# Group loads in two transfers from a six-part layout, and the maxima's transpose two places earlier, in an attention and Fourier-mixing kernel

## The chip, the cores and the metric

The kernel runs on one core of a Trainium2 chip. A core has TensorE (PE in the profile; PEld is its weight load), VectorE (DVE), ScalarE (ACT), GpSimd (POOL), and SyncE (SP), which issues the transfers; 16 DMA engines carry them out. The metric is the device time of one execution in microseconds. Before the change three runs took 1027.07, 1029.34 and 1030.61 us; the median is 1029.34.

## The reference

Two independent parts are computed and set side by side in the output (2048 rows, 2 x 576 columns, float32).

- Part A is attention with a compressive memory: 32 heads of 18 columns, 2048 positions in 4 segments of 512. In each segment there is causal softmax attention, `p = softmax(q k^T * scale + mask)`, `a_dot = p v`; from segment 1 on also a lookup in a memory matrix that the earlier segments filled, `a_mem = phi(q) M / (phi(q) z)`. The two are mixed by a gate per head, `g * a_mem + (1 - g) * a_dot`, and multiplied by `wo`. The mask is `ar[:, None] < ar[None, :]`, so a query sees keys up to its own position.
- Part B is a Fourier mixing layer on another input: `a = x Wd_re`, `b = x Wd_im` along the 576 columns, then `y = Ws_re a - Ws_im b` along the 2048 positions, with the DFT matrices given as inputs.

Float32 accuracy is kept on bfloat16 and reduced-float32 matmuls by splitting a number into a high part and remainders. In the scores, q and k are each split into three bfloat16 parts, and six of the nine products are kept: part pairs (0,0), (0,1), (1,0), (0,2), (2,0), (1,1).

## The kernel before, in words

**Projections (lines 435 to 480, about the first 230 us).** For each segment s, nine products `project_qk(s, m)` make q (m = 0 to 3) and k (m = 4 to 7) in transposed form, 128 columns at a time; m = 8 holds the last 64 columns of both. Each is split into three bfloat16 parts in a tile `p` (four buffers, L244): ScalarE makes part 0, VectorE the remainder r, ScalarE or GpSimd part 1, GpSimd part 2 (L258). One transfer writes `p` into a DRAM tensor `qd[s]` or `kd[s]` of shape 576 x 3 x 512 (L260 to L263). Then `project_v` makes v and writes it to `vd[s]`. In parallel the memory of the segment is accumulated.

**Attention with the DFT in between (L815 to L896).** From about 240 to 940 us PE works off two streams. One is attention: 128 pairs of segment and head, n = 0 to 127, four to a group G = n // 4, 32 groups, eight per segment. The other is part B's matmuls (`dense()`, L583), a stream of long accumulating products on chunks `craw` that are loaded (`c_load`, L372, four buffers), split by ScalarE into `chi` (L387) and by GpSimd into `clo` (L392).

The generator `attention()` runs over pieces p = 0 to 67. A piece takes about 10 us, handles one even and one odd pair at different stages, and is cut into eight slots by `yield`. After each slot, matmuls of the dense stream are put in until its share is level. So the order on every engine is fixed by hand: the order of the calls in the source is the order of each engine's queue, and an engine runs its queue strictly in order. `later(n, ...)` puts a call n slots on (`tick`, L84). All transfers, with `dma = nc.sync.dma_start` (recorded as L87 when put off), go through SyncE's one queue: a transfer that must wait, or that takes long to issue, holds up all behind it.

- *Stacks.* For each group two tiles hold q and k with the six part products side by side in the contraction: `qs` and `ks`, 128 partitions x 4 heads x 512, of which 6 x 18 = 108 partitions are data (`NPAIR`). There are four buffers of each. `stack_load` (L419) fills a group with 12 transfers, one for each product and side: 18 partitions x 4 heads x 1 KB, 72 KB each. In piece p, odd, after `f_turn`, it puts off the last 4 of group (p + 3) // 2, two in a slot; in an even piece the first 8 of group (p + 4) // 2 (L859 to L862). A group is first used in piece 2G.
- *Even pairs* go as: scores (`s_fill`, L683) only for each row's maximum, taken by VectorE (L680); after both even pairs of a group, `maxima` (L721) splits the maxima into three bfloat16 parts on GpSimd; `maxima_transpose` (L729) turns them on PE (`trm`), ScalarE copies the result (`mt`), and two small transfers of 3 KB, put off by one slot, write it to partitions 108 to 110 of `qs` (L735). `ks` holds ones there, so that the next score matmul (`t_fill`, L737, 111 partitions) gives transposed scores with the maximum taken off, ready for exp and for the value product. `t_fill` of a group's first even pair stands in slot 1 of piece 2G + 3, three pieces after its `s_fill`.
- *Odd pairs* are computed by rows (`f_fill`, `f_exp`), split in two fp16 parts (`f_split_hi` on ScalarE, `f_split_lo` on GpSimd and VectorE, L714), and turned by a DMA transpose (`f_turn`, L719), one in a piece, issued by SyncE as well.
- *Value products.* `pv` (L775) puts an even and an odd pair into one PSUM bank, the tag `pv` with one buffer. `pv_out` (L793) empties it with four VectorE instructions (L803 to L806) at the end of the piece; the next `pv` follows in slot 3.
- *Score banks.* PSUM tiles with the tags s and t alternate between two banks each (`bank`, L489). Before the change `trm` is one of the t tiles, so an even piece uses five of them and an odd one four.

The slots of a piece that matter here, in the order of the source: slot 0 `s_fill` 0 (L837), slot 1 `t_fill` 0 and 1 (L840), slot 2 `s_fill` 1 (L844), slot 3 in even pieces `maxima_transpose` (L848), then `pv` of the even pair (L849); slot 4 `f_fill` 1, `t_fill` 2 and in odd pieces `maxima`; slot 5 `f_turn` (L858), `stack_load`, `f_fill` 0; slot 6 `pv` of the odd pair, `f_fill` 2; slot 7 `f_exp` and `pv_out` (L874).

**Output (from about 960 us).** Part A's rows are joined, turned and multiplied by `wo` (L903 to L919).

Of the kernel before, what the change touches and what calls it, by code (L numbers as in the profile page):

```python
# [15 lines left out]
BF16 = mybir.dt.bfloat16  # L16
AF = mybir.ActivationFunctionType
OP = mybir.AluOpType
# [4 lines left out]
S, D, H, DH, NSEG, L = 2048, 576, 32, 18, 4, 512  # L23
P = 128
# [4 lines left out]
HEAD0 = [0, 7, 14, 21, 24]  # L29
NPAIR = 108  # L30
BF16_ONES = float(np.array([0x3F803F80], np.uint32).view(np.float32)[0])
QPARTS = [0, 0, 1, 0, 2, 1]
KPARTS = [0, 1, 0, 2, 0, 1]


@with_exitstack
def infini_attention_and_fnet(ctx: ExitStack, tc: tile.TileContext, xT, wqk, w8, wv, wo, beta, xtT, cT, hT, out):
    nc = tc.nc
    act, dve, pool, pe = nc.scalar, nc.vector, nc.gpsimd, nc.tensor
    dma = nc.sync.dma_start  # L40
    ctx.enter_context(tc.manual_schedule())
    const = ctx.enter_context(tc.tile_pool(name="const", bufs=1))
    dram = ctx.enter_context(tc.tile_pool(name="dram", bufs=1, space=DRAM))
    wide = ctx.enter_context(tc.tile_pool(name="wide", bufs=32))

    qd = [dram.tile([D, 3, L], BF16, name=f"qd{s}") for s in range(NSEG)]
    kd = [dram.tile([D, 3, L], BF16, name=f"kd{s}") for s in range(NSEG)]
    vd = [dram.tile([P, 4, 8, 220], BF16, name=f"vd{s}") for s in range(NSEG)]
    amd = [dram.tile([P, D], F32, name=f"amd{t}") for t in range(NT)]
    yd = [dram.tile([P, D], F32, name=f"yd{t}") for t in range(NT)]  # L50
# [30 lines left out]
    def later(n, fn, *a):  # L81
        due.setdefault(clock[0] + n, []).append((fn, a))
# [7 lines left out]
    p1, p1k = ExitStack(), ExitStack()  # L90
    sk = p1k.enter_context(tc.tile_pool(name="sb1k", bufs=1, side="right", reuse_waits="tile"))
    sb = p1.enter_context(tc.tile_pool(name="sb1", bufs=1, reuse_waits="tile"))
    ps = p1.enter_context(tc.tile_pool(name="ps1", bufs=2, space=PSUM))
# [91 lines left out]
    for i in range(2):  # L185
        kn.append(tuple(sk.tile([P, D], F32R, name=f"kn{n}{i}") for n in "hl"))
        a, b = (sk.tile([P, H, 19], F32R, name=f"vn{n}{i}") for n in "hl")
# [3 lines left out]
        t = sb.tile([P, H, 55], BF16, name=f"vs{i}")  # L191
# [29 lines left out]
    def open_qk(s):  # L221
# [4 lines left out]
        for a, b in zip(edges, edges[1:]):  # L226
# [5 lines left out]
            if s and a == 0:  # L232
                accumulate(3, (0, 1))

    def project_qk(s, m):
        if m in FIRST:
            o = FIRST.pop(m)
        else:
            o = ps.tile([P, L], F32, name="qk", tag="acc", bufs=4)
            chain(o, qk_terms(s, m))  # L240
        if m >= 4 and s < 3:
            KF[m] = sk.tile([P, L], F32, name="kf", bufs=5)
            act.activation(KF[m], o, AF.Copy)
        p = sb.tile([P, 3, L], BF16, name="p", bufs=4)  # L244
        r = sb.tile([P, L], F32, name="r", bufs=2)
        act.activation(p[:, 0], o, AF.Copy)
        dve.tensor_tensor(r, o, p[:, 0], OP.subtract)
        if s and (m < 4 or m == 8):
            n = P if m < 4 else 64
            c = m if m < 4 else 4  # L250
            phi(sb, "q", o[:n], n, pq_hi[:n, c], pq_lo[:n, c])

        def rest():
            if m in (5, 6, 7):
                pool.tensor_copy(p[:, 1], r)
            else:
                act.activation(p[:, 1], r, AF.Copy)
            pool.tensor_tensor(p[:, 2], r, p[:, 1], OP.subtract)  # L258
            if m < 8:
                later(1, dma, (qd if m < 4 else kd)[s][(m % 4) * P:(m % 4 + 1) * P], p)  # L260
            else:
                later(1, dma, qd[s][4 * P:], p[:64])
                later(1, dma, kd[s][4 * P:], p[64:])  # L263

        later(1, rest)

# [96 lines left out]
    def h_split(ri, k):  # L363
        if k == 0:
            HW[ri] = weight(wide_tile(D))
        split_wk(HW[ri], k, HRAW.pop((ri, k)), 2 * ri)
# [30 lines left out]
    qs_bufs, ks_bufs, VS = [], [], {}  # L397
# [18 lines left out]

    NG = 32

    def stack_load(G, a, b, each):  # L419
        if G < NG:  # L420
            s, g8 = divmod(G, 8)
            rows = slice(g8 * 72, g8 * 72 + 72)
            for n in range(a, b):
                c = n // 2
                buf, src, part = ((ks_bufs, kd, KPARTS[c]), (qs_bufs, qd, QPARTS[c]))[n % 2]
                later(1 + (n - a) // each, dma, buf[G % 4][18 * c:18 * c + 18],
                      src[s][rows, part, :].rearrange("(h d) t -> d h t", d=DH))

    def value_load(G):
        if G < NG:  # L430
# [4 lines left out]
    for s in range(NSEG):  # L435
        more = s < 3
        if s == 0:
            warm_up()
        open_qk(s)
        if s:  # L440
            memory()
        else:
            tick()
        for n, m in enumerate((0, 1, 2, 3, 8, 4, 5, 6, 7) if s else range(9)):
            project_qk(s, m)
            tick()
            if not more and n >= 5:
                h_split(0, n - 5)
            if s in (1, 2) and n >= 4:
                load_x(s + 1, n - 4)  # L450
            if not more and n == 0:
                for k in range(5):
                    h_load(0, k)
            if not more and n == 4:
                p1k.close()
                sr = ctx.enter_context(tc.tile_pool(name="sb2r", bufs=1, side="right", reuse_waits="tile"))
                attention_tiles()
            if not more and n == 4:
                stacks(sr, 0)
                stack_load(0, 0, 12, 2)  # L460
            if not more and n == 5:
                c_load(0)
            if not more and n == 6:
                stacks(sr, 1)
        for j in range(4):
            project_v(s, j, lookup(s, j) if s else iter(()))
            if more:
                k_natural(j)
            tick()
            for k in ((0, 1), (2, 3), (4,), ())[j] if s == 0 else ():  # L470
                load_x(1, k)
            if more and j in (1, 2):
                split_x(s + 1, j - 1)
            if not more and j < 3:
                h_split(0, 4) if j == 0 else c_cut(j - 1, dve)
            if not more:
                c_load(1 + j)
            if more and j:
                accumulate(j - 1)
# [4 lines left out]
    ps = ctx.enter_context(tc.tile_pool(name="ps2", bufs=2, space=PSUM, reuse_waits="tile"))  # L484
# [4 lines left out]
    def bank(name, shape, dtype, tag):  # L489
        turns[tag] ^= 1  # L490
        return ps.tile(shape, dtype, name=name, tag=f"{tag}{turns[tag]}", bufs=1)
# [235 lines left out]
        pool.tensor_tensor(b[:, 2], r, b[:, 1], OP.subtract)  # L727

    def maxima_transpose(G):  # L729
        t = bank("trm", [P, P], BF16, "t")  # L730
        pe.transpose(t, MB[G % 2], ident16)
        w = sa.tile([24, P], BF16, name="mt", bufs=2)
        act.activation(w, t[:24], AF.Copy)
        for h in range(2):
            later(1, dma, qs_bufs[G % 4][NPAIR:NPAIR + 3, 2 * h].rearrange("c (n t) -> c n t", n=4), w[12 * h:12 * h + 12])  # L735
# [79 lines left out]
    def attention():  # L815
        for p in range(NP + V_LAG):
            def even(lag, fn, *a):
                if 0 <= p - lag < NP:
                    fn(2 * (p - lag), *a)

            def odd(lag, fn, *a):
                if 0 <= p - lag < NP:
                    fn(2 * (p - lag) + 1, *a)

            if p < 2:
                stacks(sa, p + 2)
            if p == 0:
                value_load(0)
                stack_load(1, 0, 12, 2)
            if p % 2 == 0:  # L830
                later(39, value_load, p // 2 + 1)
            if p == NP + 1:
                o_load(0)
                o_load(1)
            even(T_LAG + 1, t_lo, 0)
            odd(F_LAG + 1, f_exp, 2)
            even(0, s_fill, 0)  # L837
            odd(F_LAG + 1, f_split_hi)
            yield SLOTS[0]
            even(T_LAG, t_fill, 0)  # L840
            even(T_LAG, t_fill, 1)
            odd(F_LAG + 1, f_split_lo, pool, 512, 1280)
            yield SLOTS[1]
            even(0, s_fill, 1)  # L844
            odd(F_LAG + 1, f_split_lo, dve, 0, 512)
            yield SLOTS[2]
            if p % 2 == 0 and 0 < p <= NP:
                maxima_transpose(p // 2 - 1)  # L848
            even(V_LAG, pv)  # L849
            even(0, s_fill, 2)  # L850
            even(T_LAG, t_mask)
            yield SLOTS[3]
            odd(F_LAG, f_fill, 1)
            even(T_LAG, t_fill, 2)
            if p % 2 and p < NP:
                maxima(p // 2)
            yield SLOTS[4]
            odd(F_LAG + 1, f_turn)  # L858
            if p % 2:  # L859
                stack_load((p + 3) // 2, 8 * (p > 1), 12, 2)  # L860
            elif p:
                stack_load((p + 4) // 2, 0, 8, 2)  # L862
            odd(F_LAG, f_fill, 0)
            even(T_LAG, t_hi)
            yield SLOTS[5]
            odd(V_LAG, pv)
            odd(F_LAG, f_fill, 2)
            odd(F_LAG, f_exp, 1)
            even(T_LAG, t_lo, 1)
            even(T_LAG, t_lo, 2)  # L870
            yield SLOTS[6]
            odd(F_LAG, f_exp, 0)
            if p >= V_LAG:
                pv_out(p - V_LAG)  # L874
            yield SLOTS[7]
# [77 lines left out]
```

## Time and profile before

| what | value |
|---|---|
| median of three runs | 1029.34 us (1027.07 to 1030.61) |
| the profiled execution | 1032.2 us, of which 1030.5 us are the span from first to last instruction |
| mean granted TensorE clock | 0.995 |
| busy: PE, DVE, ACT, POOL | 1008.0, 724.8, 714.6, 624.8 us |
| transfers | 194.26 MB, mean 189 GB/s, 16 engines busy 79.3% by the main queue |
| group loads | 192 + 192 transfers of 72 KB |
| DMA transposes | 64, one in a piece |

The page of a profile gives busy time by engine, the same in 40 equal slices of the span, the DMA queues, the chain of work that ended last (followed back from the last instruction to whatever released it), and groups of instructions by line. Further views answer who waited for whom, list instructions in order of time, and give sums for chosen stretches. In `ks<-kd` the tile on the left is written from the one on the right; SPq is SyncE's queue, and the time of an entry there is the time that the issue took, not the transfer. In square brackets stands how long the engine was idle before an instruction, and what ended it. Durations and places in time in the prediction come from the one profiled execution.

### The profile page before, as it was taken

What the parts mean: (1) busy time and instruction counts of PE and PEld (TensorE: products, weight loads), DVE (VectorE), ACT (ScalarE), POOL (GpSimd) and SP (SyncE); (2) the same over time, 40 slices, a digit from 0 to 9 for tenths busy, and PEclk for the clock granted to TensorE, in tenths of its full rate; (3) what the DMA queues carried; (4) which work ended last, traced back from release to release, by engine and by line L of the source; (5) the groups of instructions that cost most, each with busy time, mean ns of one, the idle gap of its engine ahead of it and who ended that gap; (6) DMA issues with size and microseconds to landing.
All of it is one profiled execution on the core that took longest, in us unless ns stands there. A gap on an engine that the chain in (4) does not pass through costs nothing.

```text
span 1030.5 us, 25808 instructions
## 1 busy us (share of the span) xinstructions
PE 1008.0 (98%) x9464; PEld 943.8 (92%) x9464; DVE 724.8 (70%) x1903; ACT 714.6 (69%) x1654; POOL 624.8 (61%) x668
## 2 busy tenths in 40 slices
PE   9999999999999999999999999999999989999998
PEld 8989989899999999998989899998899978999998
DVE  6645657465678777868877788887787867886442
ACT  7657575653887878777878788776777756875333
POOL 3557575765667666766666677666676755776000
PEclk9999999999999999999999999999999989999999
DMA  7516243376778999999999998799999999968574
GB/s 259 175 66 204 88 164 143 130 238 184 158 159 195 202 190 204 212 196 206 235 195 212 203 213 165 163 201 212 210 214 219 218 201 212 244 152 197 154 209 138
DMA packets 287263, 194.26 MB, mean 189 GB/s; under 512 B 210208, under 2 KB 242336, under 8 KB 287136
## 3 DMA queue, kind: packets, MB, share of 16 engines
q1 hardware_dynamic: 287136, 192.61, 79.3%
q8 instruction: 74, 1.21, 0.5%
q14 instruction: 53, 0.43, 0.1%
HBM read 106.64 MB, written 43.78 MB: 146 GB/s over the span
## 4 chain that ended last, share of the span: by engine, by line
PE 80%; DMA 8%; ACT 5%; DVE 3%; POOL 2%; issue 1%; SPq 1%; POOLq 0%; DVEq 0%; ACTq 0%
PE d L499 33%; PE s L674 6%; PE d L77 6%; PE qk L77 5%; PE qk L229 4%; PE v L77 4%; PE pv L790 4%; DMA qs<-mt 3%; PE d L544 2%; PE d L545 2%; PE d L546 2%; PE pv L791 2%; PE m L313 2%; PE look L338 1%; DMA ks<-kd 1%; PE t L748 1%
## 5 line engine op out<-in xcount | busy, mean ns | idle before, releaser
L680 DVE CUSTOM_DVE_ANT_0 s<-s,causal 128x128 f32<-128x128 f32 (+3 forms) x512 | 250.8, 500 | 112.1 <-PE s L674 98.8
L392 POOL TENSOR_TENSOR clo<-craw,chi 128x512 fp32r<-128x512 f32 x158 | 211.0, 1336 | 123.3 <-ACT chi L387 86.1
L499 PE MATMUL d<-wide,chi 128*128 128x288 f32 x1408 | 268.0, 307 | 0.0
L499 PEld LDWEIGHTS d<-wide,chi 128*128 128x128 f32 x1408 | 213.6, 190 | 2.6 <-issue 1.6
L499 PE MATMUL d<-wide,clo 128*128 128x288 f32 x704 | 178.7, 320 | 0.0
L714 POOL TENSOR_TENSOR hl<-pf,hl 128x768 f16<-128x768 f32 x64 | 115.9, 1811 | 70.6 <-ACT hl L710 59.2
L674 PE MATMUL s<-ks,qs 108*128 108x128 bf16 (+3 forms) x512 | 134.6, 305 | 9.2 <-ACT pf L703 7.4
L703 ACT ACTIVATE pf<-s,nb 128x128 f32<-128x128 f32 (+3 forms) x256 | 128.3, 527 | 6.2
L499 PE MATMUL d<-ab,chi 128*128 128x288 f32 x640 | 126.7, 307 | 0.0
L758 ACT ACTIVATE phi<-t 128x384 f16<-128x384 f32 x128 | 62.3, 487 | 91.5 <-PE t L755 91.4
L499 PEld LDWEIGHTS d<-wide,clo 128*128 128x128 f32 x704 | 119.6, 190 | 0.9
L387 ACT ACTIVATE chi<-craw 128x512 fp32r<-128x512 f32 x160 | 100.9, 631 | 24.6 <-DMA craw<-cT 14.0
L773 DVE TENSOR_TENSOR plo<-pf,phi 128x384 f16<-128x384 f32 (+1 forms) x128 | 113.8, 889 | 0.0
L759 ACT ACTIVATE pf<-t 128x384 f32<-128x384 f32 (+1 forms) x192 | 100.4, 523 | 8.5 <-PE t L748 8.4
L499 PEld LDWEIGHTS d<-ab,chi 128*128 128x128 f32 x640 | 99.4, 190 | 0.4
L710 ACT ACTIVATE hl<-pf 128x768 f16<-128x768 f32 (+1 forms) x128 | 87.4, 729 | 2.0
L499 PE MATMUL d<-ab,clo 128*128 128x288 f32 x320 | 85.6, 317 | 0.0
L544 PE MATMUL d<-wide,chi 128*128 128x288 f32 x256 | 84.2, 329 | 0.0
L545 PE MATMUL d<-wide,chi 128*128 128x288 f32 x256 | 75.6, 295 | 0.0
L546 PE MATMUL d<-wide,clo 128*128 128x288 f32 x256 | 75.5, 295 | 0.0
L714 DVE TENSOR_TENSOR hl<-pf,hl 128x512 f16<-128x512 f32 x64 | 75.2, 1175 | 0.1
L773 POOL TENSOR_TENSOR plo<-pf,phi 128x384 f16<-128x384 f32 x64 | 59.7, 933 | 16.8 <-ACT pf L759 15.9
(196 smaller groups left out, 2516.7 us busy)
## 6 DMA issues: line engine op xcount, KB each, us to landing
craw<-cT SPq DMA_DIRECT2D x128, 256.0 KB
ks<-kd SPq DMA_DIRECT2D x192, 72.0 KB
qs<-qd SPq DMA_DIRECT2D x192, 72.0 KB
craw<-xtT SPq DMA_DIRECT2D x32, 320.0 KB
out<-y SPq DMA_DIRECT2D x31, 288.0 KB
vd<-vs SPq DMA_DIRECT2D x16, 440.0 KB
vst<-vd SPq DMA_DIRECT2D x32, 220.0 KB
qd<-p SPq DMA_DIRECT2D x16, 384.0 KB
```

The costliest lines, as they stand in the source:

```text
L77: pe.matmul(o, a, b, start=n == 0, stop=n == len(terms) - 1)
L387: act.activation(hi, raw[:, :4], AF.Copy)
L392: engine.tensor_tensor(lo, raw[:, :4], hi.bitcast(F32), OP.subtract)
L499: pe.matmul(o[h], a, b[:, h * 288:h * 288 + 288], start=start, stop=stop)
L544: pe.matmul(o, xh[:, k], wl[k][:, cs], start=k == 0, stop=False)
L545: pe.matmul(o, xh[:, k], wh[k][:, cs], start=False, stop=False)
L674: pe.matmul(o[:, c:c + w], q[:, i * P:w], k[:, :w], start=True, stop=True)
L680: dve.tensor_tensor_reduce(o[:, c:c + w], o[:, c:c + w], CAUSAL[0][:, L - w:], scale=scale, scalar=-LOWEST, op0=OP.add, op1=OP.min, accum_ ...
L703: act.activation(f[:, FIRST_COL[i]:FIRST_COL[i] + w], o[:, c:c + w], AF.Exp, bias=nb[:, i:i + 1], scale=-1.0)
L714: engine.tensor_tensor(hl[:, 1, a:b], f[:, a:b], hl[:, 0, a:b], OP.subtract)
L759: act.activation(f[:, r:r + w], o[:, :w], AF.Exp, bias=LIFT, scale=SCALE)
L773: (pool if kind == 2 else dve).tensor_tensor(lo[:, a:b], f[:, a:b], hi[:, a:b], OP.subtract)
```

## The change

1. `qd` and `kd` become 576 x 6 x 512. q's parts are written in the order 0, 1, 2 to the places 0 to 2, k's in the order 2, 1, 0; the places 3 to 5 are filled by DRAM-to-DRAM copies (`copy_parts`): q gets 0, 1 and 0 again, k gets 0, 0 and 1. So place c of q and of k are again the six pairs. For m = 8, where q and k share a tile, k's three parts are written by three transfers.
2. There are four copies for 144 rows (8 heads, two groups), 64 in all. Those of segment s - 1 are issued in the projections of segment s, two after each of the first eight `project_qk`; those of segment 3 one in each even piece from 4 to 34, put off by two slots.
3. `stack_load` fills a group with two transfers of 108 partitions x 4 heads x 1 KB (432 KB each), one in each of the two slots after its call. It is called in odd pieces alone. The rows of a stack are ordered by column and then part, not by part and then column.
4. `trm` is now a tile of the tag `pv`, in the value products' bank, and `maxima_transpose` is called in slot 1, ahead of `t_fill` 0, instead of in slot 3. Its two transfers follow one slot later, as before.

```diff
-QPARTS = [0, 0, 1, 0, 2, 1]
-KPARTS = [0, 1, 0, 2, 0, 1]
+COPIES = ((0, 3, 2, 0), (1, 3, 2, 2), (0, 5, 1, 0), (1, 5, 1, 1))
+COPY_ROWS = 144
...
-    qd = [dram.tile([D, 3, L], BF16, name=f"qd{s}") for s in range(NSEG)]
-    kd = [dram.tile([D, 3, L], BF16, name=f"kd{s}") for s in range(NSEG)]
+    qd = [dram.tile([D, 6, L], BF16, name=f"qd{s}") for s in range(NSEG)]
+    kd = [dram.tile([D, 6, L], BF16, name=f"kd{s}") for s in range(NSEG)]
...
+    def copy_parts(s, n):
+        rows = slice(n // 4 * COPY_ROWS, (n // 4 + 1) * COPY_ROWS)
+        key, to, parts, at = COPIES[n % 4]
+        x = (qd, kd)[key][s][rows]
+        a = x[:, at:at + 1].to_broadcast([COPY_ROWS, parts, L]) if key and parts > 1 else x[:, at:at + parts]
+        dma(x[:, to:to + parts], a)
...
+        p0, p1, p2 = (p[:, 2 - i] if 4 <= m < 8 else p[:, i] for i in range(3))
...
-                later(1, dma, (qd if m < 4 else kd)[s][(m % 4) * P:(m % 4 + 1) * P], p)
+                later(1, dma, (qd if m < 4 else kd)[s][(m % 4) * P:(m % 4 + 1) * P, :3], p)
             else:
-                later(1, dma, qd[s][4 * P:], p[:64])
-                later(1, dma, kd[s][4 * P:], p[64:])
+                later(1, dma, qd[s][4 * P:, :3], p[:64])
+                for i in range(3):
+                    later(1, dma, kd[s][4 * P:, 2 - i], p[64:, i])
...
-    def stack_load(G, a, b, each):
+    def stack_load(G):
...
-            for n in range(a, b):
-                c = n // 2
-                buf, src, part = ((ks_bufs, kd, KPARTS[c]), (qs_bufs, qd, QPARTS[c]))[n % 2]
-                later(1 + (n - a) // each, dma, buf[G % 4][18 * c:18 * c + 18],
-                      src[s][rows, part, :].rearrange("(h d) t -> d h t", d=DH))
+            for n, (buf, src) in enumerate(((ks_bufs, kd), (qs_bufs, qd))):
+                later(1 + n, dma, buf[G % 4][:NPAIR], src[s][rows].rearrange("(h d) c t -> (d c) h t", d=DH))
...
+            if s and n < 8:
+                copy_parts(s - 1, 2 * n)
+                copy_parts(s - 1, 2 * n + 1)
...
     def maxima_transpose(G):
-        t = bank("trm", [P, P], BF16, "t")
+        t = ps.tile([P, P], BF16, name="trm", tag="pv", bufs=1)
...
             yield SLOTS[0]
+            if p % 2 == 0 and 0 < p <= NP:
+                maxima_transpose(p // 2 - 1)
             even(T_LAG, t_fill, 0)
...
             yield SLOTS[2]
-            if p % 2 == 0 and 0 < p <= NP:
-                maxima_transpose(p // 2 - 1)
             even(V_LAG, pv)
...
             if p % 2:
-                stack_load((p + 3) // 2, 8 * (p > 1), 12, 2)
-            elif p:
-                stack_load((p + 4) // 2, 0, 8, 2)
+                stack_load((p + 3) // 2)
+            elif 4 <= p < 36:
+                later(2, copy_parts, 3, (p - 4) // 2)
```

The two calls that start the first groups' loads (groups 0 and 1, L460 and L829) are shortened in the same way.

## The prediction, made before the changed kernel was run

> **What bounds the kernel now.** I read the page first: engines, then the chain that ended last.
>
> ```profile
> span 1030.5 us, 25808 instructions
> ...
> PE 1008.0 (98%) x9464; PEld 943.8 (92%) x9464; DVE 724.8 (70%) x1903; ACT 714.6 (69%) x1654; POOL 624.8 (61%) x668
> ...
> PE 80%; DMA 8%; ACT 5%; DVE 3%; POOL 2%; issue 1%; SPq 1%; POOLq 0%; DVEq 0%; ACTq 0%
> ```
>
> TensorE is the bound, and no matmul is removed. All there is to win lies in the 22.5 us (1030.5 - 1008.0) in which PE stands still, and in a lower clock afterwards. So the next view is who PE waits for.
>
> ```profile
> PE s L674 <- ACT pf L703: 7.4, 3, 4.6
> PE t L748 <- DMA qs<-mt: 6.3, 6, 1.9
> ```
>
> Two causes make 13.7 us of it: six waits for the small transfer of the maxima, and three for ScalarE. The timeline around the longest shows why ScalarE was late.
>
> ```profile
> 828.45 0.36 SPq L377 DMA_DIRECT2D craw<-cT  x1
> 833.44 0.63 ACT L387 ACTIVATE chi<-craw 128x512 fp32r<-128x512 f32 x1 [6.13 <-DMA craw<-cT]
> 834.72 0.58 PE L674 MATMUL s<-ks,qs 108*128 108x128 bf16 x2 [4.58 <-ACT pf L703]
> ```
>
> A DFT chunk was issued late, landed 5 us later, held ScalarE's in-order queue 6.13 us, and PE 4.58 us behind it. The other two (1.35 us at 533.6, 1.47 at 588.2) have a chunk landing just before (the chain shows 4.00 us from issue at 529.00 and 4.96 at 582.84). After the longest stalls the clock is halved; the windows view has:
>
> ```profile
> 792.40:794.40 2.00, 1.99 (x15) 1.66 (x13) 1.97 (x9) 1.80 (x5) 0.64 (x2) 1.00 0.74 141
> 788.00:789.00 1.00, 1.00 (x12) 1.00 (x11) 1.00 (x3) 0.80 (x3) 1.00 (x1) 1.00 1.06 386
> 832.85:839.67 6.82, 4.95 (x39) 4.80 (x39) 2.66 (x6) 4.64 (x10) 3.97 (x3) 0.50 1.16 177
> 870.39:873.80 3.41, 3.41 (x33) 3.27 (x32) 2.02 (x7) 0.91 (x3) 0.48 (x2) 0.50 0.88 197
> 890.00:930.00 40.00, 40.00 (x441) 37.77 (x440) 35.84 (x93) 32.19 (x75) 29.58 (x30) 1.00 0.80 191
> ```
>
> (columns: PE, PEld, DVE, ACT, POOL busy; granted clock; DMA share; GB/s.) Half of the 4.95 and 3.41 us of PE work was lost: 4.2 us. The last row is a stretch after the last group load (880.4): attention goes on, PE never stops.
>
> Then SyncE, which issues every transfer in order.
>
> ```profile
> L87 SPq DMA_DIRECT2D ks<-kd x192: 265/347/1856, 204.9 to 880.0; - x192
> ...
> L719 SPq DMA_TRANSPOSE ptt<-hl x64: 3022/3898/5987, 267.6 to 942.8; - x64
> ...
> L433 SPq DMA_DIRECT2D vst<-vd x32: 579/586/1701, 234.1 to 929.8; - x32
> ```
>
> (min/median/max ns on the queue.) And how it spends the time ahead of the longest maxima wait (868.99, 1.88 us):
>
> ```profile
> 853.22 4.25 SPq L719 DMA_TRANSPOSE ptt<-hl  x1
> 857.53 0.49 SPq L87 DMA_DIRECT2D ks<-kd  x1
> ...
> 863.66 1.56 SPq L87 DMA_DIRECT2D qs<-mt  x2
> ```
>
> PE had made the transpose at 859.17; SyncE reached the two transfers 4.5 us later, having gone through a 4.25 us transpose and ten more issues, and they landed 5.28 us on (the chain). The late one is SyncE's queue, not PE.
>
> **The change, step by step.** *Issues.* A group costs 12 issues of about 0.34 us (4.1 us); after, 2 with 108 partitions x 4 runs. No such row exists: bounds are a narrow load's 0.27 and its longest 1.86; I take 0.58, the row nearest in runs (vst, 128 x 4). So 1.2 us, plus half of a segment-3 copy each in the first half. The even piece loses 8 issues (2.7 us), the odd one goes from 4 narrow to 2 wide: no gain.
>
> *Transfer time.* In 792.4:794.4 only narrow loads run: 141 GB/s at share 0.74; long rows run at 386. 0.885 MB take 6.3 us at 141, 4.7 at 141/0.74, 2.3 at 386. I take 4 for the wide form. The Trainium skill (DMA: Bandwidth & Descriptors, "Why a DMA increments its semaphore by 16 and not by 1") says that a transfer uses the largest number of engines up to 16 that divides its slowest dimension: 9 for 18 rows, 12 for 108, so the wide form is still short of 16. The share of 0.74, with parts of other transfers in it, lies between 9/16 and 1 and neither proves nor refutes it. By the rule alone the group would take 6.3 x 9/12 = 4.7 us, the lump below 0.4 us more, and the sum would rise by 0.4 us at each of some four late chunks, to 1021.6. The load is now in one lump in the odd piece: 590 KB more ahead of what follows there, 1.5 us (386) to 4.2 (141); at two thirds of 4 us, 2.7.
>
> *Maxima.* In the changed order of the queue, ks, qs and one or two chunks lie between the odd piece's f_turn and the maxima's transfers, where before two pairs, chunks, od and more did. In the six waits the way from the end of f_turn to that issue was 4.4, 4.4, 5.2, 5.2, 3.5 and 6.2 us, mean 4.8; after, 2 x 0.58 plus about two issues of 0.37 and gaps, 2.0. Gain 2.8, less the lump's 2.7, plus 2.3 from the lighter even piece (2.7 less a copy's 0.4): in five of the six SyncE came to f_turn with at most 0.3 us to wait, so it was itself late. 2.4 us of gain covers every one of the six (longest 1.88): **-6.3 us**. With the lump at 4.2 the gain is 0.9, and about 1.8 us stay.
>
> *Chunks.* Ahead of the 828.45 load were eight narrow issues since 823.71: about 4 us earlier now, its 4.58 nearly gone. Ahead of 582.84 were six (2.3 us): 1.47 gone. The 529.00 load follows an odd f_turn that had waited 1.1 us for its data: nothing gained, and the lump can add up to 2.7. I remove **-7.4** and put back **+2.5** for that one and others of its kind (the chunks issued right behind an odd f_turn at 706, 748 and 771 had 3.8 to 4.4 us from issue to use). Clock: **-4.2**.  The Trainium skill (TensorE: Matmul & The Clock Gate, Part 1) has the clock halved after an idle window of about 3.4 us; here 1.88 us of idle at 867 went before a half-clock stretch, so the trace disagrees, and by the page's rule only the first dip (2.5 us) would go with its gap, which makes the sum 1.7 us higher.
>
> *Start of attention.* PE waited 0.47 us for ks at 248.8; its load (245.52) stood behind twelve narrow issues since 234.8: **-0.5**.
>
> *The pv bank.* The transpose moves two slots up and must now wait until pv_out of the piece before has read the bank. Behind it on PE stands everything. The trace has both ends: og (L806) ends, then the first t_fill of the even piece starts, which is the new place. At 828.95 against 829.57 there is room; at 856.55 against 856.41 there is not, nor at 703.31 against 702.38. Over the 32 even pieces seven are short, by 0.42, 0.32, 0.32, 0.94, 0.14, 0.27 and 0.10 us, 2.5 in all; another 0.06 us from DVE's end to PE's start (266.10 to 266.16) for some eight. **+3.0**; the bounds are 0, if DVE gains as the stalls go, and 0.94 x 32 = 30. The maxima on POOL (L727) end 2.3 us or more ahead of that place, so they hold nothing. ScalarE's copy (0.27 us) moves, the count stays. The t banks alternate more evenly; the piece with five becomes four, no wait shows there now, nothing counted.
>
> *Copies.* 48 of 64 run in the projections (0.15 to 0.29 MB each, 10.6 MB over 175 us, 61 GB/s); 60:175 had DMA share 0.38, 135 GB/s and PE busy 115.00 of 115: cover enough, as attention sustains 204. The last 16 lie in pieces 4 to 34: 0.6 to 1.6 us of transfer each by 386 and 141 GB/s, twice that if reading and writing don't overlap. The m = 8 k rows go in three transfers instead of one, 0.68 us more issue; ScalarE already waits 1.89 us for kd at 207 and PE loses 0.6 right behind it. **+0.7**, bounds 0 and 6 (2 us in each of three segments).
>
> Sum from the profiled execution's own time: 1032.2 - 6.3 - 7.4 - 4.2 - 0.5 + 2.5 + 3.0 + 0.7 = **1020.0 us**. That execution lies 2.9 us above the median of 1029.34, which I read as more stalls than usual; what is left after the change has few of them, so I take 1020 for the median too: -0.9%.
>
> **Rivals.** (a) *The wide lump holds up the small transfer* (slower). qs<-mt lands 4.0 to 5.3 us after issue now. If the lump runs at the narrow form's rate (+4.2) and f_turn starts no earlier because POOL sets it, landing is later by 4.2 - 2.8 = 1.4 us than now. In most groups the use comes 4 to 6 us after the issue, so some 18 of the 30 with loads ahead would wait, by about 1.2 us each: +22 on the forecast, **1042**. It decides once the lump takes over 2.8 us without an earlier f_turn. For: the queue runs in order at share 0.97 over 400:800. Against: narrow loads are what runs slowest. (b) *The pv bank becomes the pace.* With PE no longer stalling, DVE falls 0.45 us further behind, which eats the usual room of 0.3 to 0.5: 0.4 us in each of 32 pieces, +13 less 3, **1030**, no change. Against: DVE idles 22% of attention. (c) *The chunks' stalls stay*: they come in odd pieces too, where SyncE gains nothing. Then 4 of the 7.4 and half of the clock return: **1026**. (d) *The change doesn't do what it says*: wide issues block as the longest narrow one did (1.86); two of them make 3.7 us against 4.1, SyncE gains nothing, and only the earlier place of the maxima is left: -6.3, +3.0, +0.7, **1029**.
>
> **The numbers.** Forecast 0.66; (c) 0.11, just faster; (b) 0.07 and (d) 0.06, no change; (a) 0.10, slower. About 0.3% is what a measurement of this kernel can tell from no change, 1026.3 to 1032.4. Faster 0.77, same 0.13, slower 0.10. The forecast alone reaches from 1012 (no new wait, little put back) to 1025; with (b), (c) and (d) the range is **1011 to 1031**.
>
> **What would show it.** Right: the qs<-mt waits under 1 us in all; ks<-kd and qs<-qd x32 at about 0.6 us of issue; stretches of 1 KB loads well over 141 GB/s; no clock of 0.50 in mid-span; a new PE wait, trm <- DVE og, of about 3 us. Wrong: trm waits over 10 us, t_fill still behind qs<-mt, wide issues over 1.5 us, or gaps between 60 and 235 us for the copies.

## The result, and the profile after

The changed kernel takes a median of **1023.18 us** (1019.78 to 1024.5, eight runs) against 1028.24 us (1024.19 to 1030.61, eight runs) before: ratio **0.995**, 95% interval 0.9928 to 0.9972. It is faster, by 0.5% and not by the 0.9% foretold. Run again beside other kernels, it took 1022.62 us (1019.34 to 1024.97, twelve runs), ratio 0.9958 (0.9941 to 0.9976).

Its profiled execution took 1024.34 us; before's took 1032.2. The page of the changed kernel, with the span, the engines and the chain:

```profile
span 1022.6 us, 25516 instructions
...
PE 1007.7 (99%) x9464; PEld 944.0 (92%) x9464; DVE 727.8 (71%) x1903; ACT 711.4 (70%) x1654; POOL 626.1 (61%) x668
...
PE 84%; DMA 4%; DVE 4%; ACT 3%; POOL 3%; issue 2%; POOLq 0%; SPq 0%; DVEq 0%; ACTq 0%
```

PE is busy as long as before (1007.7 and 1008.0), and stands still for 14.9 us (1022.6 - 1007.7) instead of 22.5. DMA fell from 8% of the chain to 4%. For whom PE waits (total, times, longest):

```profile
PE v L79 <- DVE vr L304: 3.4, 1, 3.4
PE m L324 <- POOL knl L205: 2.4, 3, 1.8
PE trm L742 <- DVE og L817: 2.2, 5, 0.9
```

The same two waits of the projections before:

```profile
PE v L77 <- DVE vr L293: 0.9, 1, 0.9
PE m L313 <- POOL knl L203: 0.2, 1, 0.2
```

Neither of the two rows of before that the prediction shows is left: no wait for `qs<-mt`, none for ScalarE's `pf`. In their place stand the pv bank (`trm`, 2.2 us) and the two rows of the projections, which have grown. The windows of the same kernel (PE, PEld, DVE, ACT, POOL busy; clock; DMA share; GB/s):

```profile
170.32:173.73 3.41, 3.41 (x17) 3.41 (x16) 2.36 (x3) 1.67 (x4) 2.75 (x3) 0.50 0.23 87
231.76:235.17 3.41, 3.41 (x18) 3.41 (x17) 2.42 (x5) 1.41 (x4) 2.66 (x2) 0.50 0.80 276
400.00:800.00 400.00, 398.43 (x4296) 374.19 (x4296) 330.01 (x925) 315.22 (x755) 275.31 (x294) 1.00 0.88 213
60.00:175.00 115.00, 112.76 (x710) 102.53 (x709) 62.03 (x128) 68.89 (x149) 75.80 (x79) 0.99 0.59 196
```

and two of them before:

```profile
60.00:175.00 115.00, 115.00 (x749) 105.33 (x748) 65.54 (x136) 72.45 (x157) 76.85 (x80) 1.00 0.38 135
400.00:800.00 400.00, 392.27 (x4217) 367.66 (x4215) 321.20 (x907) 311.66 (x742) 269.92 (x288) 1.00 0.97 204
```

Attention is what the change was expected to make of it: in 400:800 PE is busy 398.43 us (392.27 before), at full clock. The projections are not. In 60:175 PE was busy all 115.00 us before and is now for 112.76, and the two stretches of half clock, in mid-attention before, now lie at 170 and 232 us, each just behind a gap. PE's gaps in the projections add up to 6.3 us (1.5 before), the largest being 0.44 us at 108.31, 1.80 at 167.66 and 3.45 at 226.91.

What is late there? GpSimd's order of time ahead of the gap at 167.66:

```profile
157.58 1.42 POOL L205 TENSOR_TENSOR knl<-ke,knh 128x576 fp32r<-128x576 f32 x1 [0.46 <-DVE knh L204]
165.68 1.17 POOL L364 TENSOR_TENSOR am<-nd,w 128x576 f32<-128x576 f32 x1 [6.68 <-DMA amd<-am]
...
168.01 1.40 POOL L205 TENSOR_TENSOR knl<-ke,knh 128x576 fp32r<-128x576 f32 x1
```

The tile `am` has one buffer. Its next use waits until the transfer of the one before, `amd<-am`, has left it: GpSimd stands 6.68 us, and `knl`, for which PE's memory product waits, comes that much later. That transfer, issued behind copies, took 7.16 us from 158.35 in the chain that ended last. In the 2.4 us from `am`'s end at 155.90 to that issue SyncE also waited three times, 0.85 us together, for earlier transfers to land, two of them copies: its issues take turns on eight semaphores, and each waits until the transfer eight issues before it has landed. The same chain in the last segment (start, time, what):

```profile
214.16 8.50 DMA qd<-qd
...
222.72 6.49 DMA vd<-vs
...
229.32 0.43 ACT vs L301
...
230.36 2.59 PE v L79 x14
```

`qd<-qd` is one of the new copies; `vd<-vs`, issued behind them, takes 6.49 us, and ScalarE, VectorE and PE follow one after the other. In before nobody waited for `amd<-am`; now GpSimd does for 18.0 us in three waits. For `vd<-vs` ScalarE waits 14.9 us in four waits (3.6 in two before). By the mean share (0.59 in 60:175) the DMA engines have room for the copies. In the stretch that matters they have none: while `amd<-am` was on its way the share was 1.02, where the same stretch had 0.36 before (changed kernel first):

```profile
158.00:164.00 6.00, 6.00 (x55) 6.00 (x54) 3.79 (x11) 3.48 (x8) 0.99 (x1) 1.00 1.02 386
158.00:164.00 6.00, 6.00 (x53) 6.00 (x52) 4.93 (x12) 3.80 (x9) 3.83 (x4) 1.00 0.36 139
```

### The profile page after: what moved, and what is told of

Read it like the earlier page. It is cut to its first block, busy times and chain, and to the rows that moved or that the text cites. A ratio compares the mean times of both kernels' runs of the same rounds, so it can differ in the third digit from the quotient of the medians.

```text
span 1022.6 us, 25516 instructions
## 1 busy us (share of the span) xinstructions
PE 1007.7 (99%) x9464; PEld 944.0 (92%) x9464; DVE 727.8 (71%) x1903; ACT 711.4 (70%) x1654; POOL 626.1 (61%) x668
## 3 DMA queue, kind: packets, MB, share of 16 engines
q8 instruction: 74, 1.21, 0.5%
## 4 chain that ended last, share of the span: by engine, by line
PE 84%; DMA 4%; DVE 4%; ACT 3%; POOL 3%; issue 2%; POOLq 0%; SPq 0%; DVEq 0%; ACTq 0%
PE d L510 38%; PE s L685 7%; PE d L79 6%; PE pv L801 4%; PE qk L231 4%; PE qk L79 3%; PE d L555 3%; PE d L556 3%; PE d L557 3%; PE v L79 3%; PE pv L802 2%; PE t L759 1%; POOL p L268 1%; DMA amd<-am 1%; PE m L324 1%
## 5 line engine op out<-in xcount | busy, mean ns | idle before, releaser
L784 DVE TENSOR_TENSOR plo<-pf,phi 128x384 f16<-128x384 f32 (+1 forms) x128 | 118.2, 923 | 0.0
```

The source lines that it names most:

```text
L784: (pool if kind == 2 else dve).tensor_tensor(lo[:, a:b], f[:, a:b], hi[:, a:b], OP.subtract)
```

## The experiments

The theory from this profile: (1) the wide loads free SyncE's queue, and that alone takes away the stalls of attention; (2) the earlier transpose adds the pv wait and gives nothing once SyncE is in time; (3) the copies cost several microseconds in the projections, by where they stand, not by their bytes. The rivals: the earlier transpose is what removes the `qs<-mt` waits; or it is the wide loads' faster transfer, not their fewer issues. Kernels run together share one median of before: 1025.07 us (13 runs) for the first four below; 1026.21 (17) for the kernel with five empty issues and the changed kernel run again; 1025.19 (12) for the other four.

**The transpose alone.** The kernel before, with part 4 of the change:

```diff
-        t = bank("trm", [P, P], BF16, "t")
+        t = ps.tile([P, P], BF16, name="trm", tag="pv", bufs=1)
...
             yield SLOTS[0]
+            if p % 2 == 0 and 0 < p <= NP:
+                maxima_transpose(p // 2 - 1)
             even(T_LAG, t_fill, 0)
...
-            if p % 2 == 0 and 0 < p <= NP:
-                maxima_transpose(p // 2 - 1)
             even(V_LAG, pv)
```

> The kernel before with part 4 alone: the maxima's transpose in the value products' bank, in slot 1; narrow loads. If SyncE's queue is what made things late (mine), the two small transfers move up by no more than an od and a chunk issue, 1 to 1.5 us: of the 6.3 us of qs<-mt waits 2 to 4 stay, the chunk waits of 7.4 us and the halved clock stay, and the pv bank costs its 2.2: 1026 to 1030 beside 1028.2, no change. If the earlier place is what matters (rival), no qs<-mt wait is left and the time is near 1023.

Measured: 1031.33 us (1029.53 to 1036.07), ratio 1.0066 (1.004 to 1.0093): slower. PE's waits in this kernel:

```profile
PE s L674 <- ACT pf L703: 6.6, 6, 2.7
PE pv L790 <- DMA ptt<-hl: 3.2, 3, 2.3
PE trm L731 <- DVE og L806: 2.1, 4, 0.9
...
PE t L748 <- DMA qs<-mt: 1.1, 1, 1.1
```

The `qs<-mt` waits do fall from 6.3 to 1.1 us. But SyncE has as much to issue as ever: ScalarE's lateness stays, another transfer (`ptt<-hl`, 0.3 before) is now late, and the pv bank asks 2.1. With one item moved forward in a queue as late as before, others are late. These rows come to about as much as those of before's profiled execution, which at 1032.2 us lay above all 13 runs of before here; they say where PE waits, and do not add up to the 6 us between the medians, whose cause is not shown. The rival's 1023 falls, and no change was too mild as well. Rival (d)'s remainder, "only the earlier place" at 1029 against 1032.2, would have been a gain, and there is none.

**The loads alone.** The changed kernel, with part 4 undone (`trm` a t tile again, in slot 3).

> The changed kernel with the transpose put back in slot 3 and the t bank. Mine: with wide loads SyncE waits for the transpose and not the other way round, so the small transfers go out some 2.5 us later than in the changed kernel and still land in time (about 9 us from transpose to use there): no qs<-mt wait over 1 us in all, no pv wait, 1021, 2 us under the changed kernel. Rival: without the earlier place the qs<-mt waits are back, 4 to 6 us and a clock dip, 1028.

Measured: 1019.08 us (1016.67 to 1021.91), ratio 0.9935 (0.9914 to 0.9956). No `qs<-mt` wait and no pv wait is left; in the projections the gaps stay (4.33 us at 224.56, 1.01 at 108.52). The wide loads remove the maxima's wait with the transpose where it was.

**The copies where nothing small follows.** The changed kernel, with the 16 copies of a segment issued at once, right behind `open_qk(s)`:

```diff
-            if s and n < 8:
-                copy_parts(s - 1, 2 * n)
-                copy_parts(s - 1, 2 * n + 1)
...
         open_qk(s)
         if s:
+            for n in range(16):
+                copy_parts(s - 1, n)
             memory()
```

> The changed kernel with the 16 copies of a segment issued at once right after the first products of the next segment, in the stretch where the transfer queue is near empty, not two after each projection. Mine: the gaps of 0.4, 1.8 and 3.4 us at 108, 168 and 227 and the two half-clock stretches come from copies queued ahead of the memory results (am, one buffer) and of v; all go but the 0.85 that was there before: 1015 to 1018. Rival: the sheer volume of the copies (10.6 MB) costs the time wherever it stands; the waits move to the q rows' writes and the x loads: 1021 to 1024.

Measured: 1017.22 us (1016.71 to 1018.46), ratio 0.9924 (0.9903 to 0.9945). The same copies of the same bytes: the wait of GpSimd for `amd<-am` is gone, the clock is 1.0 throughout, and of the projections' gaps 3.1 us are left, where 0.85 was expected; so the place costs most of it, and part of the gaps stays with the copies moved. The runs lie within 1.8 us of each other, where those of the changed kernel spread over 4.7.

**The earlier transpose in its old bank.** The changed kernel, with `trm` a t tile in slot 1.

> The changed kernel with the transpose in slot 1 but in the t bank as before. Mine: t_fill 1 now takes the bank that the transpose has just filled and must wait for ScalarE's copy of it, 0.3 to 0.6 us in each of 32 even pieces, against 2.2 us of pv waits saved: 1031 to 1040, slower than the changed kernel. Rival: ScalarE is done in time as it idles before that copy; then the pv bank was the dearer place, and the time is 1021.

Measured: 1048.37 us (1043.65 to 1050.51), ratio 1.0216 (1.0188 to 1.0244). One row of PE's waits tells why:

```profile
PE t L762 <- ACT mt L744: 22.1, 23, 2.1
```

A transpose right ahead of `t_fill` takes a bank that `t_fill` needs, and ScalarE must empty it first: about 1 us, 23 times. So the pv bank was the right one for slot 1, at 2.2 us instead of 22.1. The direction was as expected, the size larger.

**Both: loads alone, copies early.** The second and third kernel joined.

> The wide loads with the copies in the quiet stretch, and the transpose in its old place and bank (the two gains so far without the pv wait). If the pv wait (2.2 us) and the copies' place (about 6 us of gaps and half clock) are separate, they add up: 1014 to 1016, two under the kernel with quiet copies alone. If the earlier transpose is needed once the rest is fast (rival), qs<-mt waits show and it stays at 1017 or above.

Measured: **1013.71 us** (1012.83 to 1014.46), ratio **0.9874** (0.9845 to 0.9902): better than both kernels. Its windows:

```profile
60.00:75.00 15.00, 15.00 (x76) 12.64 (x75) 5.36 (x9) 6.57 (x14) 9.21 (x16) 1.00 0.90 283
400.00:800.00 400.00, 399.92 (x4314) 376.09 (x4313) 331.95 (x929) 316.63 (x756) 276.47 (x296) 1.00 0.87 214
```

A segment's copies fill the DMA engines to 0.90 for 15 us, and PE loses nothing, since nothing that it needs soon is behind them. In attention PE is busy 399.92 of 400 us. PE's waits in its view add up to 4.8 us.

**Empty issues put back.** The last kernel, with ten tiny transfers for each group (18 partitions x 4 heads x 16 B, read and never used), two in the odd piece and eight in the even one, where the narrow loads stood:

```diff
                 stack_load((p + 3) // 2)
+                idle_load((p + 3) // 2, 0, 2)
-            elif 4 <= p < 36:
-                later(2, copy_parts, 3, (p - 4) // 2)
+            else:
+                idle_load((p + 4) // 2, 2, 10)
+                if 4 <= p < 36:
+                    later(2, copy_parts, 3, (p - 4) // 2)
```

> The kernel e7_loads_quiet with ten more transfers for each group, of 18 partitions x 4 runs x 16 bytes (12 KB for each group's ten, read and never used), where the narrow loads stood: SyncE issues as many transfers as in the kernel before, while hardly a byte is added. If the number of issues made things late (mine), SyncE is 3 to 4 us later in each even piece and the waits for qs<-mt and for the chunks come back in good part: 1020 to 1026. If it was the slow transfer of the narrow loads (rival), nothing comes back: 1014 to 1017.

Measured: 1047.34 us (1044.8 to 1052.47), ratio 1.0206 (1.0172 to 1.0241).

```profile
PE t L767 <- DMA qs<-mt: 20.9, 12, 3.3
```

With next to no bytes added, the issues bring the waits back. Of the 31.8 us between the spans of the two profiled executions 24.4 are waits (20.9 for `qs<-mt`, the rest behind ScalarE's `pf` and `ptt<-hl`), and some 5.8 are half clock (13.65 us at 0.50, PE busy in 11.7 of them).

That it is 34 us in the medians, more than was expected, and slower than the kernel before at nearly the same issue time of SyncE in 240:940 (575 us of 700; 568.6 before), fits what becomes of the small transfers. For the 30 groups that have loads ahead of them, the medians are:

| kernel | from the end of the transpose on PE to the first small issue | from the end of the last group load's issue to that | from that to both landed |
|---|---|---|---|
| before | 2.03 us | 2.25 | 4.16 |
| the changed kernel | 0.71 | 2.52 | 4.21 |
| without the empty issues | 0.35 | 4.71 | 2.93 |
| with ten empty issues | 2.03 | 2.69 | 5.91 |

SyncE comes to them as late as before, and so close behind a wide load that they take longer to land: rival (a) of the prediction, which the changed kernel did not show. SyncE now also waits for the wide loads to land, since an empty issue takes one of the eight places like any other. Of its waits here (first the issue of `f_turn`, then those that were put off):

```profile
SPq L738 <- DMA qs<-qd: 13.4, 8, 2.6
SPq L89 <- DMA ks<-kd: 10.4, 15, 1.8
```

All waits of SyncE for landings in 240:940 are 35.8 us here, 5.7 without the empty issues and 37.6 before. What the issues' own time costs and what the eight places cost was not tested apart.

**Half of them.** Five empty issues for each group, one in the odd piece and four in the even one.

> The kernel e9_idle_issues with five idle transfers for each group instead of ten: one in the odd piece, four in the even. SyncE issued for 466 of the 700 us from 240 to 940 with none and for 575 with ten; five make some 520. If there is a level that SyncE must stay under, past which every wait adds up (mine now, as ten cost 33 us and not the 6 to 12 foretold), five cost far less than half: 1014 to 1020. If each issue costs its share of the time (rival), 1030.

Measured: 1013.85 us (1013.47 to 1014.23), ratio 0.9868 (0.9845 to 0.9891): no cost at all, with SyncE issuing 496 us of the 700 and waiting 10.1 us for landings. Five cost nothing, ten cost 34 us. In this order of the work the queue's slack is used up somewhere between 496 and 575 us of 700; no run lies between.

**Fewer DMA engines for a load.** The best kernel, with each wide load cut in two of 54 partitions in the same slot:

```diff
-                later(1 + n, dma, buf[G % 4][:NPAIR], src[s][rows].rearrange("(h d) c t -> (d c) h t", d=DH))
+                x = src[s][rows].rearrange("(h d) c t -> (d c) h t", d=DH)
+                for a, b in zip((0, 54, 108), (0, 54, 108)[1:]):
+                    later(1 + n, dma, buf[G % 4][a:b], x[a:b])
```

> The kernel e7_loads_quiet with each wide load cut in two of 54 partitions, two issues in a slot: four issues a group. By the Trainium skill's rule on the number of engines (DMA: Bandwidth & Descriptors) 54 rows run on 9 engines as 18 did. If the narrow loads' slow transfer was the cause (rival), the 1 KB stretches run near 190 to 220 GB/s instead of well over that, and waits of some us come back: 1018 to 1024. If the issues were (mine), two more a group cost about 0.7 us of SyncE that it has to spare: 1014 to 1017.

Measured: 1016.36 us (1014.26 to 1020.48), ratio 0.9903 (0.9871 to 0.9936).

**More of them.** The same, cut at 96 instead of 54.

> The same cut at 96 instead of 54: by the same rule 96 rows run on all 16 engines and 12 on 12, against 12 for the uncut 108. If the rate of the group loads still matters, it is 0.5 to 2 us under e7_loads_quiet; if there is no wait left on what stands behind them (mine), it is the same within 1 us, and only the rate in the 1 KB stretches differs.

Measured: 1013.41 us (1013.03 to 1013.64), ratio 0.9872 (0.9831 to 0.9913).

These two vary the transfer's rate with two issues more for each group. In a stretch where group loads alone run, the four forms show (each a window of one kernel): before, 18 partitions,

```profile
459.20:460.20 1.00, 1.00 (x10) 1.00 (x9) 0.93 (x6) 0.71 (x2) 0.45 (x1) 1.00 0.54 133
```

the kernel with 54,

```profile
822.20:823.20 1.00, 1.00 (x10) 1.00 (x8) 1.00 (x5) 1.00 (x3) 1.00 (x1) 1.00 0.62 184
```

the best kernel with 108,

```profile
441.70:442.70 1.00, 1.00 (x12) 0.93 (x11) 1.00 (x3) 1.00 (x4) 1.00 (x1) 1.00 0.81 274
```

and the one with 96.

```profile
677.60:678.60 1.00, 1.00 (x12) 0.93 (x12) 1.00 (x4) 1.00 (x3) 0.76 (x1) 1.00 0.99 316
```

In these four windows the rate goes from 133 to 316 GB/s. Over all such stretches the medians are 148, 177, 261 and 221, so 96 keeps more engines at work and is not the fastest form. The kernel with parts of 54 is within 3 us of the best one, with intervals that overlap, although its small transfers land 5.33 us after their issue (2.93 in the best kernel); 96 wins nothing more; ten empty issues cost 34 us. So what the wide form brings to this kernel is above all fewer issues, and its faster transfer is hardly needed. A kernel with few issues at the narrow loads' own rate was not run.

**The changed kernel again**, beside the kernel with five empty issues.

> The changed kernel once more, unaltered, on the same chip as the other one of this pair, so that the kernels made from it are compared with it and not only with the kernel before. Both theories: 0.993 to 0.997 of the kernel before, with executions in two bunches some 4 us apart if the half-clock stretches in the projections come in some executions and not in others.

Measured: 1022.62 us, as told above. The profiled execution, at 1020.24 us, shows PE gaps of 0.84, 1.45 and 2.73 us in the projections and no half clock, where the first profile had two such stretches. So single executions differ by what the copies do to the projections. Why the gaps differ was not settled; which of them halves the clock goes by where they fall in time (last section). Nor was `am` with two buffers tried.

## Why the prediction was right, and where it was not

The forecast was faster, at 1020.0 us and -0.9%, in a range of 1011 to 1031. The time came out faster, inside the range, 3.2 us above the forecast. Step by step, from the profiled executions (1032.2 and 1024.34):

| step | foretold | measured |
|---|---|---|
| waits for `qs<-mt` | -6.3 | -6.3, none left |
| chunks held up, PE behind ScalarE | -7.4, put back +2.5 | -7.4, nothing put back |
| half clock in attention | -4.2 | -4.2 |
| `ks` at the start of attention | -0.5 | -0.5 |
| pv bank | +3.0 | +2.2 (5 waits) |
| copies in the projections | +0.7 | **+8.3** |
| sum | -12.2 | -7.9 |

- *The queue.* The issues of the wide loads have a median of 0.54 us for `ks` and 0.45 for `qs`; 0.58 was taken. SyncE's issue time in 240:940 fell from 568.6 to 470.6 us, and from the start of the transpose on PE to the issue of its first small transfer it now takes 0.94 us in the median (2.17 before). (The prediction's 859.17 is such a start as well; that transpose ended at 859.40, so SyncE came 4.3 us after it and not 4.5.) That SyncE "was itself late" shows in where it has time now: of the 700 us it issues nothing in 229 (131 before), and it stands waiting for 105 us ahead of the 64 issues of `f_turn` (19 before), 81 of them for VectorE and 22 for PE. That the number of issues did it is shown by ten empty ones bringing the waits back; that the rate had little part, by loads in parts of 54 at 184 GB/s not doing so, down to that rate.
- *The lump.* Its delay was priced at 2.7 us for late chunks, and 2.5 put back for it. None was seen in this profile (one chunk cost 0.98 us in the kernel with the copies moved), which fits SyncE arriving early enough for the lump ahead of a chunk to be carried before the chunk is due. Rival (c) falls with it, and (d) with the issue times. Rival (a) falls for this kernel: the small transfers land 4.21 us after their issue, as before (4.16), and come earlier. Its mechanism is real all the same, as the ten empty issues show.
- *The pv bank.* The small shortfalls read from before, 2.5 us plus 0.5, became 2.2; VectorE did not fall further behind, so rival (b) falls. The step was right, but what it buys is nothing here: without part 4 the loads gave 0.9935 instead of 0.9958, 2.4 us by the ratios and about the wait itself, though the intervals overlap a little. With the copies moved the same step is clearer: 1013.71 us without part 4 and 1017.22 with it, and the runs of the two do not overlap. The prediction gave the `qs<-mt` gain to lighter SyncE and earlier place together; the lighter SyncE was enough.
- *The copies: the step that failed*, by its size. The mechanism was named, gaps between 60 and 235 us, but it was priced at the issue time on SyncE and at the DMA's free share: "cover enough, as attention sustains 204". The bounds of 0 to 6 were not wide enough for this execution. Gaps in that stretch were one of the prediction's own signs of being wrong. A mean share says whether the bytes fit, and not how long a short transfer waits behind them; here 6.49 us for `vd<-vs`, against 4.32 in before's chain at 217.73. At three places PE came to stand behind it: 4.85 us more of gaps, and 3.4 us of half clock (two stretches of 3.41 us of work at half speed). In the second profile of the changed kernel, without the half clock, the term is about 4. Moving the copies recovered most of it.
- *From the profiled execution to the median.* The execution of before at 1032.2 us stood above every one of its eight runs (1024.19 to 1030.61). The prediction read the 2.9 us over the median as more stalls than usual and still took 1020 for the median, on the ground that what is left has few stalls. That holds only if no new ones come; the copies brought new ones. The medians moved by 5.1 us, the profiled executions by 7.9.
- *Luck.* The copies were priced 7.6 us too low. The 2.5 us put back for late chunks, which did not come, and the pv bank's 0.8 made up for 3.3 of them, so the forecast of the profiled execution missed by 4.3 (1024.34 against 1020.0). That these errors had opposite signs was luck; the gains in attention themselves came as foretold.

## What to carry to other kernels

Where one queue issues everything, count its issue time in the stage, and how long it stands waiting for data: where it waited long (234 us of 700 without issues in the best kernel) five issues more for a group were free, and where it did not (131 before, 125 with ten empty issues) what stood behind was late. Moving one late transfer ahead in such a queue only made another one late here; take issues away. Price a bulk copy by the short transfers that are issued behind it and by whoever waits for their landing, not by the DMA's mean share over a long stretch, and put it where none follows.

## What the runs showed of the hardware

- Group loads of 1 KB rows keep a share of the DMA engines that goes by their partitions. Over all stretches of 0.8 us in 240:940 of which 98% of the bytes are such rows (63 to 90 in each kernel), the median share was 0.55 with 18, 0.59 with 54, 0.78 with 108 and 1.03 with 96. By the rule of the Trainium skill (DMA: Bandwidth & Descriptors, "Why a DMA increments its semaphore by 16 and not by 1") these use 9, 9, 12 and 16 engines, which is 0.56, 0.56, 0.75 and 1.00: the traces agree, which the share of 0.74 in the prediction could not decide. The rate does not go by the share alone: its medians in these stretches were 148, 177, 261 and 221 GB/s.
- Half clock came behind gaps of 1.80 and 1.88 us, for 3.41 us where PE was busy, and did not come behind one of 2.73 us in the second profile of the changed kernel. The length of the gap alone does not decide it. In each of the six traces that have more than one stretch at 0.50 these begin on one grid of 3.41 us, and those ahead of the last matmul last one or two of its steps. Among all steps at full clock in the twelve traces, from 7 us on and up to the last matmul, the twelve in which PE stood still for 1.80 us or more in sum (up to 3.41) were followed by half clock, and none was in which it stood still for 1.74 or less. The gap of 1.80 us lay within one step; the one of 2.73, from 225.12, fell on two, 1.21 us on the first and 1.52 on the second.
- A tiny transfer (16 B pieces) takes 0.33 us of SyncE, a wide load of six times as many pieces, 1 KB each, 0.45 to 0.54: here an issue costs mostly by being one.
